# Other places for the tokens' tiles and the weights in the second mixture of experts

## The chip, the cores and the metric

The kernel runs on one core of one Trainium2 chip. What is measured is the device time of one execution, in microseconds (us). The kernel before was run three times; one further execution was profiled, and every row shown here is from that one.

## The reference

Three layers follow one another on 2304 tokens of width 512. The first is attention with a compressive memory, the second a soft mixture of experts, the third a mixture whose gate is balanced by eight rounds of row and column scaling. The change lies in the third, cut here to its core:

```python
P = np.exp(logits - logits.max())        # logits = x @ w_gate, 2304 x 8
for _ in range(8):
    P /= P.sum(1, keepdims=True) + 1e-09
    P /= P.sum(0, keepdims=True) + 1e-09
    P *= N / E
for e in range(8):
    h = np.maximum(x @ w1[e], 0.0)       # 2304x512 @ 512x1024
    out += P[:, e:e + 1] * (h @ w2[e])   # 2304x1024 @ 1024x512
```

## The kernel before

The input `x` of the third layer has rank 32 (it is a mixture of 32 slots), so `layer1` makes the hidden layer of 256 tokens with eight matmuls (L1043, `l<-c4T,a`). Eight experts with nine groups of 256 tokens each are 72 units of work. The first six of expert 0 (`RAW = 6`) go through `plain` (L1327), which multiplies 512 columns at a time, and the other 66 units go through `product`.

In `product` the second matrix product of a unit is done by a Strassen-like scheme: seven products instead of eight, in the order p5, p1, p7, p6, p2, p3, p4. Each takes one token tile (`s1`, `a11`, `s3`, `s2`, `a12`, `s4`, `a22`) and one weight tile (`T1`, `B11`, `T3`, `T2`, `B21`, `B22`, `T4`; the `B` tiles and `T3` lie in the big tiles `BB1` and `BB2`). Each number is split into a high and a low float32r part, names ending in h and l, so a product is 4 steps over the inner dimension times 3 matmuls: high by high (L1360), high by low (L1361), low by high (L1362). That is 84 matmuls of 128x256 for a unit. In each of them the token tile is the stationary operand (loaded by an LDWEIGHTS, which reads 128 columns or 512 bytes of each partition) and the weights are the moving operand (256 columns or 1024 bytes of each partition). The steps of a product lie 512 and 1024 bytes apart, so all 12 matmuls of a product have one and the same distance between their two operands, taken by the remainder by 512.

Places are given out one after another inside a pool: `mA` holds `BB1` and the `T1` and `T2` of even experts, `mB` the token tiles, `mS` small tiles of the gate, `mC` the `T1` and `T2` of odd experts, `BB2` and `T4`, and `mD` the first layer's tiles `a4`. A tile that nobody uses (name "gap") moves all tiles that come after it. The engines' order is written out by hand (`manual_schedule`), and nothing in it depends on places.

Of the kernel before, what the change touches and what calls it, by code (L numbers as in the profile page):

```python
# [8 lines left out]
F32 = mybir.dt.float32  # L9
# [12 lines left out]
def infini_attention_soft_moe_sinkhorn_moe(  # L22
# [22 lines left out]
    P = 128  # L45
# [826 lines left out]
    mA = ctx.enter_context(tc.tile_pool(name="mA", bufs=1, reuse_waits="tile"))  # L872
    mB = ctx.enter_context(tc.tile_pool(name="mB", bufs=1, reuse_waits="tile"))


    mS = ctx.enter_context(tc.tile_pool(name="mS", bufs=1, reuse_waits="tile"))
    mS.tile([P, 24], F32, name="gap")
    mC = ctx.enter_context(tc.tile_pool(name="mC", bufs=1, reuse_waits="tile"))
    mD = ctx.enter_context(tc.tile_pool(name="mD", bufs=1, reuse_waits="tile"))
    ps_l = ctx.enter_context(tc.tile_pool(name="ps_l", bufs=1, space=PSUM, reuse_waits="tile"))  # L880
# [152 lines left out]
    accB = mB.tile([P, NU, DM], F32, name="accB")  # L1033
    accD = mB.tile([P, NU, CW], F32, name="accD")
    units = [(e, u) for e in range(E) for u in range(NU)]
    X, Y, PH, FU = {}, {}, {}, {}

    def layer1(g):
        e, u = units[g]
# [12 lines left out]
    def h_tile(g, nm, z):  # L1052
        if (g, nm, z) not in X:
            tag = ("s3" if nm == "a21" else nm) + z
            X[g, nm, z] = mB.tile([P, KH, P], F32R, tag=tag, name=nm + z)
        return X[g, nm, z]

# [13 lines left out]
    def h_hi(g, nm):  # L1071
        a = nm[0] == "a"
        nc.scalar.activation(  # L1073
            out=h_tile(g, nm, "h"), in_=ph(g, nm) if a else FU[g, nm], func=AF.Relu if a else AF.Copy
        )

    def h_lo(g, nm):
        hi, lo = h_tile(g, nm, "h").bitcast(F32), h_tile(g, nm, "l")
        if nm[0] == "a":
            nc.vector.scalar_tensor_tensor(  # L1080
                out=lo, in0=ph(g, nm), scalar=0.0, in1=hi, op0=ALU.max, op1=ALU.subtract
            )
        else:
            nc.gpsimd.tensor_tensor(out=lo, in0=FU[g, nm], in1=hi, op=ALU.subtract)  # L1084
# [451 lines left out]
```

## Time and profile before

| | |
|---|---|
| median of 3 runs | 1152.31 us (1148.59 to 1152.92) |
| profiled execution, its own time | 1150.51 us |
| its span, first to last instruction | 1148.7 us |
| TensorE (PE) busy | 1096.2 us, 95% of the span |
| VectorE (DVE), ScalarE (ACT), GpSimd (POOL) busy | 853.0, 656.6, 658.7 us |

The profiled execution's own time is 1.8 us above its span and 1.8 us below the median of the three runs. PE's busy time counts matmuls whose ends are modelled and which overlap one another, so how closely they follow each other is read from their starts or their number in a stretch, not from the busy share. The first mixture and the attention end at about 320 us, the six plain units at about 400 us, and the 66 units of seven products fill the rest.

### The profile page before, as it was taken

The page shows a single profiled execution, that of the slowest core. Times are in us where ns is not written, and L with a number is a line of the kernel's source. Part 1 is how long each engine was busy: PE and PEld are TensorE (multiplying, and loading weights), DVE is VectorE, ACT ScalarE, POOL GpSimd, SP SyncE. Part 2 cuts the span into 40 slices and gives each one's busy share as a digit, 9 for nine tenths or more (in the row PEclk, how much of TensorE's full clock was granted, in tenths as well). Part 3 has the DMA queues.
Part 4 walks back from the last instruction along what each step waited for, and adds up shares of the span by engine and source line. Part 5 has one row for each costly group of instructions (what it writes and reads, how often), then busy time and mean ns, then how long its engine had stood idle before and what let it go on. Part 6 is the DMA issues. An engine that isn't in the chain of part 4 may idle for free.

```text
span 1148.7 us, 24354 instructions
## 1 busy us (share of the span) xinstructions
PE 1096.2 (95%) x9247; PEld 992.6 (86%) x9247; DVE 853.0 (74%) x1870; ACT 656.6 (57%) x1423; POOL 658.7 (57%) x602
## 2 busy tenths in 40 slices
PE   5899899988999998999999999999999999999998
PEld 4778777773377888999999999999999999999998
DVE  6888888875146556678778868877887787788776
ACT  6888878751233388556555644655564465556442
POOL 5433323300333287577767857776785877678665
PEclk9999999997999999999999999999999999999999
DMA  6677777238822004001300400120040012000111
GB/s 163 197 205 232 203 224 203 74 123 361 353 74 74 1 2 147 2 2 42 107 2 1 148 2 1 56 93 1 1 148 1 1 68 80 2 1 6 55 53 55
DMA packets 37411, 102.31 MB, mean 89 GB/s; under 512 B 6448, under 2 KB 13232, under 8 KB 33200
## 3 DMA queue, kind: packets, MB, share of 16 engines
q1 hardware_dynamic: 36864, 100.69, 27.1%
q8 instruction: 73, 1.20, 0.4%
q14 instruction: 42, 0.34, 0.1%
q10 hardware_dynamic: 432, 0.09, 0.0%
HBM read 96.04 MB, written 4.72 MB: 88 GB/s over the span
## 4 chain that ended last, share of the span: by engine, by line
PE 71%; DVE 13%; ACT 9%; issue 3%; DMA 2%; POOL 2%; SPq 0%; DVEq 0%; ACTq 0%; POOLq 0%
PE y L1360 15%; PE y L1362 15%; PE y L1361 15%; PE y L1327 5%; PE l L1043 5%; PE po L436 3%; DVE f L1067 2%; PE ph L830 2%; ACT sm L360 2%; PE pt L399 1%; PE pa L999 1%; DVE sm L356 1%; DMA kd<-in_k_dram 1%; DVE a22l L1080 1%; PE pc L1227 1%
## 5 line engine op out<-in xcount | busy, mean ns | idle before, releaser
L1067 DVE SCALAR_TENSOR_TENSOR f<-l,f 128x512 f32<-128x512 f32 x264 | 181.5, 688 | 57.2 <-ACT a11h L1073 50.1
L1084 POOL TENSOR_TENSOR s1l<-f,s1h 128x512 fp32r<-128x512 f32 x66 | 88.5, 1341 | 157.2 <-ACT s1h L1073 153.2
L1376 DVE TENSOR_TENSOR accA<-accA,y 128x512 f32<-128x512 f32 (+1 forms) x129 | 86.7, 672 | 49.2 <-PE y L1362 43.2
L1073 ACT ACTIVATE a12h<-l 128x512 fp32r<-128x512 f32 x72 | 43.2, 600 | 94.0 <-PE y L1362 90.4
L1084 POOL TENSOR_TENSOR s4l<-f,s4h 128x512 fp32r<-128x512 f32 x66 | 85.9, 1302 | 17.4 <-ACT s4h L1073 16.4
L1376 DVE TENSOR_TENSOR accB<-accB,y 128x512 f32<-128x512 f32 x129 | 88.4, 686 | 6.7 <-PE y L1362 1.2
L1084 POOL TENSOR_TENSOR s2l<-f,s2h 128x512 fp32r<-128x512 f32 x66 | 86.1, 1304 | 0.8 <-ACT s2h L1073 0.8
L1043 PE MATMUL l<-c4T,a 128*128 128x256 f32 x576 | 79.0, 280 | 7.5 <-DVE a22l L1080 6.6
L1084 POOL TENSOR_TENSOR s3l<-f,s3h 128x512 fp32r<-128x512 f32 x66 | 85.7, 1299 | 0.3 <-ACT s3h L1073 0.3
L360 ACT ACTIVATE sm<-sm,mn 128x128 f32<-128x128 f32 (+3 forms) x128 | 71.0, 556 | 17.8 <-DVE mn L356 16.3
L1043 PEld LDWEIGHTS l<-c4T,a 128*128 128x128 f32 x576 | 71.6, 188 | 10.4 <-DVE a22l L1080 8.8
L1360 PE MATMUL y<-T2h,s2h 128*128 128x256 f32 x264 | 76.4, 289 | 0.0
L1063 ACT ACTIVATE f<-l 128x512 f32<-128x512 f32 x66 | 39.1, 592 | 65.3 <-PE l L1043 61.9
L969 POOL TENSOR_TENSOR BB1l<-raw,BB1h 128x512 fp32r<-128x512 f32 x32 | 41.1, 1297 | 58.8 <-ACT BB1h L963 55.1
L1361 PE MATMUL y<-BB2l,s4h 128*128 128x256 f32 x264 | 73.8, 279 | 0.3 <-DVE BB2l L969 0.3
L1360 PE MATMUL y<-BB2h,a12h 128*128 128x256 f32 x264 | 73.8, 279 | 0.0
L1362 PE MATMUL y<-BB1h,s3l 128*128 128x256 f32 x264 | 73.3, 278 | 0.1
L1361 PE MATMUL y<-T2l,s2h 128*128 128x256 f32 x264 | 73.4, 278 | 0.0
L1362 PE MATMUL y<-T2h,s2l 128*128 128x256 f32 x264 | 73.3, 278 | 0.0
L1360 PE MATMUL y<-BB2h,s4h 128*128 128x256 f32 x264 | 73.2, 277 | 0.0
L1360 PE MATMUL y<-T4h,a22h 128*128 128x256 f32 x264 | 73.2, 277 | 0.0
L1361 PE MATMUL y<-T4l,a22h 128*128 128x256 f32 x264 | 73.2, 277 | 0.0
(314 smaller groups left out, 4236.1 us busy)
## 6 DMA issues: line engine op xcount, KB each, us to landing
wm<-in_moe_w_dram SPq DMA_DIRECT2D x32, 1024.0 KB, 8.1
raw<-in_moe_w_dram SPq DMA_DIRECT2D x32, 512.0 KB, 4.2
w<-in_moe_w_dram SPq DMA_DIRECT2D x32, 512.0 KB, 4.3
qd<-in_q_dram SPq DMA_DIRECT2D x30, 288.0 KB, 4.2
kd<-in_k_dram SPq DMA_DIRECT2D x30, 288.0 KB, 4.7
qp<-in_q_dram SPq DMA_DIRECT2D x16, 288.0 KB, 3.0
vt<-in_v_dram SPq DMA_DIRECT2D x16, 256.0 KB, 2.7
out_dram<-accB SPq DMA_DIRECT2D x18, 128.0 KB, 1.8
```

Of the source, the lines that this page charges most:

```text
L360: nc.scalar.activation(out=sm[:, 0:n], in_=sm[:, 0:n], func=AF.Exp, scale=-1.0, bias=mnc, accum_out=X.sums[:, i, h : h + 1],)
L969: eng(g).tensor_tensor(out=w_tile(e, nm, "l")[:, h], in0=full(e, nm, i), in1=w_tile(e, nm, "h")[:, h].bitcast(F32), op=ALU.subtract,)
L1043: nc.tensor.matmul(ph[:, f, :], a4s[e][:, P * (KH * j + f) : P * (KH * j + f) + P], c4T[:, UT * u : UT * u + UT], start=True, stop=True,)
L1063: nc.scalar.activation(out=f_tile(g, nm), in_=ph(g, nm), func=AF.Relu)
L1067: nc.vector.scalar_tensor_tensor(out=f_tile(g, nm), in0=ph(g, src), scalar=0.0, in1=b, op0=ALU.max, op1=op)
L1073: nc.scalar.activation(out=h_tile(g, nm, "h"), in_=ph(g, nm) if a else FU[g, nm], func=AF.Relu if a else AF.Copy)
L1084: nc.gpsimd.tensor_tensor(out=lo, in0=FU[g, nm], in1=hi, op=ALU.subtract)
L1327: nc.tensor.matmul(Y[g, i], X[g, f"a{i}{j}", "hhl"[n]][:, f, :], BB[j, "hlh"[n]][:, f].rearrange("p a c -> p (a c)"), start=j == 1 and f = ...
L1360: nc.tensor.matmul(o_, hh[:, f, :], wh[:, f, :], start=f == 0, stop=False)
L1361: nc.tensor.matmul(o_, hh[:, f, :], wl[:, f, :], start=False, stop=False)
L1362: nc.tensor.matmul(o_, hl[:, f, :], wh[:, f, :], start=False, stop=f == KH - 1)
L1376: nc.vector.tensor_tensor(out=acc, in0=acc, in1=y, op=ALU.add)
```

## The change

One unused tile of 96 bytes in `mS` is taken away, and five unused tiles are put between the token tiles: 32 bytes ahead of `s3h`, `a22h`, `s2h` and `s4h`, 128 bytes ahead of `s1h`. Tiles that come later in `mB` move by 32 to 256 bytes, and those of `mS`, `mC` and `mD` by 160.

```diff
-
     mS = ctx.enter_context(tc.tile_pool(name="mS", bufs=1, reuse_waits="tile"))
-    mS.tile([P, 24], F32, name="gap")
...
-    X, Y, PH, FU = {}, {}, {}, {}
+    X, Y, PH, FU, GAPS = {}, {}, {}, {}, {}
...
             tag = ("s3" if nm == "a21" else nm) + z
+
+            n = {"s3h": 32, "a22h": 32, "s1h": 128, "s2h": 32, "s4h": 32}.get(tag, 0)
+            if n and tag not in GAPS:
+                GAPS[tag] = mB.tile([P, n // 4], F32, name=f"gap_{tag}")
             X[g, nm, z] = mB.tile([P, KH, P], F32R, tag=tag, name=nm + z)
```

No engine's row of instructions changes: kinds, order, shapes and semaphore waits are the same, only addresses differ. The addresses give these distances (address of the moving operand less that of the stationary one, remainder by 512 bytes):

| product and operands | before | after |
|---|---|---|
| p5: T1, s1 | 448 | 256 (even experts), 416 (odd) |
| p1: BB1, a11 | 448 | 448 |
| p7: BB1, s3 | 448 | 416 |
| p6: T2, s2 | 448 | 224 (even), 384 (odd) |
| p2: BB2, a12 | 448 | 64 |
| p3: BB2, s4 | 448 | 352 |
| p4: T4, a22 | 448 | 32 |
| first layer: c4T, a4 | 448 | 288 |
| plain units: a11, a21, a12, a22 | 448 | 448, 416, 64, 32 |

In the matmuls that spread the slots (L1025, L1026) the distances were 0, 128, 256 and 384 before and are 96, 224, 352 and 480 after. In the attention nothing moves; there the operands of L354 and L355 stand 0 apart for the first head of a block and 256 for the second, and those of L340 64 or 320.

## Rows read from the trace of the kernel before

**Rows 1.** The page's busy times, granted clock by slice, and chain that ended last.
```profile
PE 1096.2 (95%) x9247; PEld 992.6 (86%) x9247; DVE 853.0 (74%) x1870; ACT 656.6 (57%) x1423; POOL 658.7 (57%) x602
...
PEclk9999999997999999999999999999999999999999
...
PE 71%; DVE 13%; ACT 9%; issue 3%; DMA 2%; POOL 2%; SPq 0%; DVEq 0%; ACTq 0%; POOLq 0%
```

**Rows 2.** Waits of PE from 464 us on: us in total, times, longest.
```profile
PE l L1043 <- DVE a22l L1080: 1.0, 6, 0.2
```

**Rows 3.** Stretches of one expert each, PE alone.
```profile
664.00:764.00 100.00, 99.84 (x888) 1.00 0.14 44
...
1064.00:1149.00 85.00, 81.47 (x692) 0.99 0.15 51
```

**Rows 4.** Two stretches of 40 us, PE alone.
```profile
676.00:716.00 40.00, 40.00 (x355) 1.00 0.01 1
...
1068.00:1108.00 40.00, 40.00 (x342) 1.00 0.16 54
```

**Rows 5.** L1361 in 676:716: duration ns least/median/most.
```profile
L1361 PE MATMUL y<-BB1l,s3h x16: 276/276/276, 677.1 to 709.4; 128*128 128x256 f32 x16
```

**Rows 6.** The same line in 1068:1144.
```profile
L1361 PE MATMUL y<-BB2l,s4h x31: 281/281/281, 1068.0 to 1143.7; 128*128 128x256 f32 x31
```

**Rows 7.** PE's groups of the whole span, shapes apart: busy us, mean ns.
```profile
L1043 PE MATMUL l<-c4T,a 128*128 128x256 f32 x576 | 79.0, 280 | 7.5 <-DVE a22l L1080 6.6 <-DVE a L66 0.9
...
L1360 PE MATMUL y<-T4h,a22h 128*128 128x256 f32 x264 | 73.2, 277 | 0.0
...
L1327 PE MATMUL y<-BB1h,a21l 128*128 128x512 f32 x24 | 9.6, 399 | 0.0
```

**Rows 8.** PE in order of time (start us, us), the first layer after a wait.
```profile
661.47 0.28 PE L1361 MATMUL y<-BB1l,a11h 128*128 128x256 f32 x1
661.58 0.28 PE L1362 MATMUL y<-BB1h,a11l 128*128 128x256 f32 x1
662.02 1.21 PE L1043 MATMUL l<-c4T,a 128*128 128x256 f32 x8 [0.16 <-DVE a22l L1080]
663.07 0.28 PE L1360 MATMUL y<-BB1h,s3h 128*128 128x256 f32 x1
663.18 0.28 PE L1361 MATMUL y<-BB1l,s3h 128*128 128x256 f32 x1
663.30 0.28 PE L1362 MATMUL y<-BB1h,s3l 128*128 128x256 f32 x1
```

**Rows 9.** The same view, the spreading of the slots.
```profile
674.21 0.28 PE L1025 MATMUL p<-ahi,sel 128*128 128x256 f32 x1
674.33 0.28 PE L1026 MATMUL p<-alo,sel 128*128 128x256 f32 x1
674.44 0.28 PE L1025 MATMUL p<-ahi,sel 128*128 128x256 f32 x1
674.56 0.28 PE L1026 MATMUL p<-alo,sel 128*128 128x256 f32 x1
674.67 0.29 PE L1360 MATMUL y<-BB1h,a11h 128*128 128x256 f32 x1
```

**Rows 10.** The same view, scores of one block of the attention.
```profile
70.86 0.35 PE L354 MATMUL ps<-kh,qh 128*128 128x256 f32 x1
71.05 0.28 PE L355 MATMUL ps<-klz,qh 128*128 128x256 f32 x1
71.17 0.28 PE L354 MATMUL ps<-kh,qh 128*128 128x256 f32 x1
71.29 0.28 PE L355 MATMUL ps<-klz,qh 128*128 128x256 f32 x1
```

**Rows 11.** L1360 in 464:1064: duration ns least/median/most.
```profile
L1360 PE MATMUL y<-BB1h,a11h x216: 276/276/286, 474.6 to 1061.4; 128*128 128x256 f32 x108
```

**Rows 12.** PE's groups of the first 250 us: 512 columns in the attention.
```profile
L340 PE MATMUL ps<-klz,qx 128*128 128x512 f32 x32 | 10.0, 394 | 0.0
```

## The prediction

> **What bounds the kernel now.** I read the page first: PE is busy for 95% of the span, and 71% of the chain that ended last is its own work; the granted clock is at the higher of its two levels (2.4 GHz) but for short stretches [rows 1]. The waits of PE come next, since the places of tiles can only matter where PE does not stand still for another reason: from 464 us to the end it waits 1.0 us in all, for VectorE [rows 2]. An expert takes 100.00 us, of which PE is busy for 99.84 [rows 3]. So from there on the time is the number of matmuls by the distance in time from one to the next, and nothing else.
>
> That distance is therefore what the other views were read for. Of two stretches of 40 us, one shows 355 matmuls and the other 342 [rows 4]. A matmul is shown for some 280 ns and overlaps those behind it, so a stretch also counts those that began up to 280 ns ahead of it, about 2.4 of them: 40,000 / 352.6 is 113.4 ns from start to start, and 40,000 / 339.6 is 117.8 ns. Both stretches do the same products with the same distance 448 at the same granted clock. The shown duration follows: 276 ns for all 16 of a group in the first stretch, 281 for all 31 of a group in the second [rows 5, 6], and every other group there reads the same. The shown duration less 163 ns is the step, so rows that give only a mean duration tell which of two levels a group was on. I call 113.4 the low level and 117.8 the high one; they are 4.4 ns apart, or 3.9%.
>
> The reader is to see two things in this. The level is no property of the distance alone, because 448 shows both. And it lasts: the second stretch is 40 us without a change. Which level follows is set where the stream is broken. Before L1043 waits for VectorE the steps are 113 ns; behind the wait the eight matmuls of L1043 take 1.05 us to the next product (the first, after the pause, longer than the others), and the starts of the products go on 0.11 and 0.12 apart, on the high level [rows 8].
>
> **The change, part by part.** No instruction, wait or transfer is added, removed or put elsewhere. The gaps themselves cost nothing: they are addresses that nobody writes. What can change is the step of PE's matmuls, and I cost each group by levels.
>
> 1. The seven products: 66 units by 84 matmuls are 5,544, in 21 groups of 264, one of which is shown [rows 7]. Their mean shown duration is 277 ns in that group and in most others (73.2 us by 264 is 277.3), between one fifth and one quarter of the 5 ns from the low to the high level, so I put 0.23 of them on the high level now. Three of the 21 groups, those of p1, keep distance 448; 18 groups, 4,752 matmuls, get another. No stretch of the trace runs long at another distance with 256 columns, so the price has bounds from both sides. From below: all 4,752 on the low level, 4,752 x 0.23 x 4.4 ns = 4.8 us gained. From above by the levels that last: all on the high level, 4,752 x 0.77 x 4.4 = 16.1 us lost. Still further, there is a third step: the longest of the ordinary matmuls in L1360 shows 286 ns, 123 from start to start [rows 11]. It shows singly, not in stretches; all 4,752 there would lose 4,752 x (122.8 - 114.4) = 40 us.
>
> The nearest rows for other distances are short ones with 256 columns. The spreading of the slots has distances 256, 128, 0 and 384, and its starts are 0.12, 0.11, 0.12 and 0.11 us apart [rows 9]. In the attention the second head of a block (distance 256) takes 0.12 us from L354 to L355, and the first head (distance 0) takes 0.12 from L355 to L354; the 0.19 us of the first L354 is the change of operand kind behind the transposes, not the distance, since L355 at distance 0 does not have it [rows 10]. So of the four kinds of neighbour three lie at the high level or a little above, and one (L1026) nearer the low one. I take three quarters of the moved matmuls on the high level and one quarter on the low one: 4,752 x (0.75 - 0.23) x 4.4 = 10.9 us lost. Against these rows speaks that they are short and stand just behind a break, where 448 too shows the high level; that is why the bound below stays in.
>
> 2. The first layer, 576 matmuls, goes from 448 to 288. Its mean of 280 holds about a dozen long ones behind waits [rows 7]; I put 0.4 of it on the high level now, and three quarters later: 576 x 0.35 x 4.4 = 0.9 us. Ends: 1.0 gained, 1.5 lost.
>
> 3. The plain units: 216 of 288 matmuls with 512 columns move. They show 399 [rows 7], the attention's with 512 columns at distances 64 and 320 show 394 [rows 12]. That is 5 ns at most by 216, 1.1 us gained, and as much lost if it goes the other way; I take nothing.
>
> 4. VectorE, ScalarE and GpSimd read and write the moved tiles. Their durations lie beside PE's work, with at least 20% of each expert idle on the fullest of them by the page's busy shares (VectorE 74% of the span) [rows 1]; a few ns there are hidden. If PE is slower, they have more room, so PE's wait of 1.0 us [rows 2] can only shrink.
>
> The sum is 10.9 + 0.9 = 11.8 us on the profiled execution's 1150.5, which gives 1162.3. The median of the runs shown lies 1.8 us above that execution, so the forecast for the median is 1164.
>
> **A rule of the Trainium skill, weighed.** The Trainium skill's page "SBUF — State Buffer" (Who interferes with whom) gives TensorE two independent read ports for SBUF, one for the moving operand and one for the weight load, and says that PE never waits on anyone. By it no distance could cost anything and the time would stay at 1152. This trace does not bear the second half out fully: the same instructions at the same granted clock show two lasting steps, 113.4 and 117.8 ns [rows 4]; something in reading or loading does cost time, but which operands collide is not shown here, nor that their distance decides.
>
> **The rivals.** *No change.* The level is set by where the stream is broken and by what broke it, and the distance only shifts in time where two reads meet; the stream settles again to the same step. For it: 448 has both levels, and breaks choose between them [rows 8]. Against it: the two levels exist at all, and a product at another distance has to settle anew seven times a unit. The time is 1152, with 3 us either way. The Trainium skill's page "SBUF — State Buffer" leads to the same.
>
> *Faster.* The new distances keep every stretch on the low level, also the last expert, which now lies high to its end [rows 6]. The place is the 66 units, the price 4.8 + 1.0 = 5.8 us, so 1146. It decides if fewer than 0.23 of the moved matmuls are high. Against it: three of four neighbours. No row with 256 columns goes below about 113 ns, so I see no larger gain. [...]
>
> *Much slower.* Some distances put a product on the third step, which is now seen singly [rows 11]. Half of the moved matmuls there and half on the high level: 40 / 2 + 16 / 2 = 28 us, so about 1180; all there 1192. It decides from a third of the moved products on.
>
> **How the numbers follow.** The forecast, between half and all of the moved matmuls on the high level (1158 to 1170), has a chance of 0.50; no change 0.26, faster 0.09, much slower 0.15. About 0.5%, or 5.8 us, is what a measurement of this kernel can tell from no change. Faster by more than that takes nearly the whole of the gain in reach: 0.07. Within it lie the no-change rival, the rest of faster and a small piece of the forecast: 0.31. Slower by more: 0.62. The range for 8 in 10 leaves out most of faster below and the worse half of much slower above: 1148 to 1180.
>
> **What would show it.** If the steps are right, the stretches of one expert grow from 100.0 us to about 101.7 (756 matmuls, 648 of them moved, by 2.3 ns), the last stretch stays nearly as it is, the groups of p1 keep about 277 ns while the moved groups show 279 to 281, and PE still waits for nobody. Groups at 276 throughout with experts of 99 us would show the faster rival; groups at 285 and more the third step. All groups at 277 with both levels in the same places would show that the distance does nothing. The prediction is wrong if a moved group shows a step that no row here has, above 123 or below 113 ns, or if p1 changes as much as the moved groups, since then the neighbours in the stream, not the own distance, set the level.

## The result and the profile after

The changed kernel takes 1166.47 us (median of 4 runs, 1166.0 to 1166.96), the kernel before on the same chip 1151.12; the ratio is 1.0127, with a 95% interval of 1.0102 to 1.0153. The forecast was 1164, in a range of 1148 to 1180, so the way and about the size were right. The profiled execution has a span of 1164.3 us against 1148.7.

The page of the changed kernel, busy time and chain, as in [rows 1]:

```profile
PE 1114.4 (96%) x9247; PEld 1014.6 (87%) x9247; DVE 847.4 (73%) x1870; ACT 656.3 (56%) x1423; POOL 659.0 (57%) x602
...
PEclk9999999997999999999999999999999999999999
...
PE 82%; DVE 8%; ACT 6%; issue 2%; POOL 1%; DMA 1%; SPq 0%; DVEq 0%; ACTq 0%; POOLq 0%
```

The number of instructions and the granted clock are as before; only PE and its weight loads are busy for longer, and PE's share of the last chain rose from 71% to 82%. From 464 us on PE waits for nobody any more (1.0 us before, [rows 2]).

One stretch of 102 us, close to a whole expert, and three of 40 us, PE alone, as in [rows 3, 4]:

```profile
667.00:769.00 102.00, 102.00 (x884) 1.00 0.13 43
...
676.00:716.00 40.00, 40.00 (x342) 1.00 0.01 1
776.00:816.00 40.00, 40.00 (x341) 1.00 0.01 1
1096.00:1136.00 40.00, 40.00 (x342) 1.00 0.16 52
```

The stretch that held 355 matmuls holds 342, and the two others hold 341 and 342: 40,000 / 339.6 is 117.8 ns from start to start, and from the first expert to the last no unit averages less than 117.6. From the start of one expert's first product to the next it is 102.7 us (the starts in the trace, 653.06 to 1063.70 us for four experts), where it was 100.0.

PE's groups of the whole span, busy us and mean ns; each product's high-by-low matmuls (L1363 now, L1361 before), one more row of p1, and the first layer:

```profile
L1041 PE MATMUL l<-c4T,a 128*128 128x256 f32 x576 | 79.6, 280 | 5.5 <-DVE a22l L1082 4.6 <-DVE a L66 0.9
...
L1363 PE MATMUL y<-BB2l,s4h 128*128 128x256 f32 x264 | 74.8, 283 | 0.1
...
L1363 PE MATMUL y<-T1l,s1h 128*128 128x256 f32 x264 | 74.3, 282 | 0.0
...
L1363 PE MATMUL y<-T2l,s2h 128*128 128x256 f32 x264 | 74.1, 281 | 0.0
...
L1363 PE MATMUL y<-BB1l,s3h 128*128 128x256 f32 x264 | 74.0, 280 | 0.0
...
L1363 PE MATMUL y<-BB2l,a12h 128*128 128x256 f32 x264 | 73.7, 279 | 0.0
L1362 PE MATMUL y<-BB1h,a11h 128*128 128x256 f32 x264 | 73.7, 279 | 0.0
L1363 PE MATMUL y<-T4l,a22h 128*128 128x256 f32 x264 | 73.7, 279 | 0.0
...
L1363 PE MATMUL y<-BB1l,a11h 128*128 128x256 f32 x264 | 73.5, 278 | 0.0
```

The groups rose from about 277 [rows 7] to 278 to 283, p1 (`a11`) too, whose distance is unchanged. (The one group that reads more, p6's first matmuls behind the transposes, rose from 289 to 293.) The wait in L1041 fell from 6.6 us in eleven places to 4.6 in five.

How a product's matmuls follow one another shows in order of time. Here is p1 in one unit of an odd expert of the changed kernel (start us, us):

```profile
690.65 0.28 PE L1362 MATMUL y<-BB1h,a11h 128*128 128x256 f32 x1
690.77 0.28 PE L1363 MATMUL y<-BB1l,a11h 128*128 128x256 f32 x1
690.88 0.29 PE L1364 MATMUL y<-BB1h,a11l 128*128 128x256 f32 x1
691.01 0.28 PE L1362 MATMUL y<-BB1h,a11h 128*128 128x256 f32 x1
691.12 0.28 PE L1363 MATMUL y<-BB1l,a11h 128*128 128x256 f32 x1
691.24 0.28 PE L1364 MATMUL y<-BB1h,a11l 128*128 128x256 f32 x1
691.35 0.28 PE L1362 MATMUL y<-BB1h,a11h 128*128 128x256 f32 x1
691.47 0.28 PE L1363 MATMUL y<-BB1l,a11h 128*128 128x256 f32 x1
691.58 0.28 PE L1364 MATMUL y<-BB1h,a11l 128*128 128x256 f32 x1
```

The first five steps are 0.12, 0.11, 0.13, 0.11 and 0.12 (114 to 123 ns in the unrounded starts, 118 on average); from the sixth on they are 113 to 114, the low level, to the last but one. Behind p5 at 416, p1 pays for its neighbour's distance in its first matmuls and then settles. In even experts, where p5 stands at 256, it does not settle:

```profile
598.77 0.28 PE L1362 MATMUL y<-BB1h,a11h 128*128 128x256 f32 x1
598.89 0.28 PE L1363 MATMUL y<-BB1l,a11h 128*128 128x256 f32 x1
599.01 0.28 PE L1364 MATMUL y<-BB1h,a11l 128*128 128x256 f32 x1
...
599.84 0.28 PE L1362 MATMUL y<-BB1h,a11h 128*128 128x256 f32 x1
599.95 0.28 PE L1363 MATMUL y<-BB1l,a11h 128*128 128x256 f32 x1
600.07 0.28 PE L1364 MATMUL y<-BB1h,a11l 128*128 128x256 f32 x1
```

In 27 of the 30 units of even experts p1's steps are 117 to 119 ns up to its last matmul: it lies on the high level of 448 throughout. Its mean is 117.6 in even experts and 115.4 in odd ones (113.6 and 114.5 before). The other products do not reach the low level: p3 (352) repeats 117, 125, 115, 124, 118, 121 to its end, p2 (64) 117 and 118, p4 (32) 118, 120, 113, 116. p7, at 416 in all experts, has two patterns, with a mean of 118.8 in even experts and 117.4 in odd ones.

Below, a product's step is the mean from one start to the next over its matmuls, worked out from the starts in the trace without steps of 140 ns or more (change of operand kind, waits); a quiet unit is one without transposes, spreading or waits in it. Before, the steps of p5, p1, p7, p6, p2, p3 and p4 are 114.4, 114.1, 114.3, 114.9, 114.2, 114.2 and 114.4 (mean 114.37); after, 119.2 in even and 118.9 in odd experts, 116.4, 118.0, 118.0 and 118.8, 117.9, 119.7 and 116.9 (mean 118.06).

### The profile page after: what moved, and what is told of

It reads as the page before. It is cut to its first block, busy times and chain, and to the rows that moved or that the text cites. A ratio compares the mean times of both kernels' runs of the same rounds, so it can differ in the third digit from the quotient of the medians.

```text
span 1164.3 us, 24354 instructions
## 1 busy us (share of the span) xinstructions
PE 1114.4 (96%) x9247; PEld 1014.6 (87%) x9247; DVE 847.4 (73%) x1870; ACT 656.3 (56%) x1423; POOL 659.0 (57%) x602
## 4 chain that ended last, share of the span: by engine, by line
PE 82%; DVE 8%; ACT 6%; issue 2%; POOL 1%; DMA 1%; SPq 0%; DVEq 0%; ACTq 0%; POOLq 0%
PE y L1362 18%; PE y L1364 18%; PE y L1363 18%; PE l L1041 6%; PE y L1329 5%; PE po L436 3%; PE ph L830 2%; ACT sm L360 2%; PE pt L399 2%; PE pa L997 1%; PE pso L848 1%; DVE sm L356 1%; PE pc L1229 1%; PE pma L449 1%; DVE r L463 1%
## 5 line engine op out<-in xcount | busy, mean ns | idle before, releaser
L1041 PE MATMUL l<-c4T,a 128*128 128x256 f32 x576 | 79.6, 280 | 5.5 <-DVE a22l L1082 4.6
L1041 PEld LDWEIGHTS l<-c4T,a 128*128 128x128 f32 x576 | 73.0, 188 | 7.2 <-DVE a22l L1082 5.6
L1363 PE MATMUL y<-BB2l,s4h 128*128 128x256 f32 x264 | 74.8, 283 | 0.1
L1364 PE MATMUL y<-BB2h,s4l 128*128 128x256 f32 x264 | 74.6, 283 | 0.0
L1362 PE MATMUL y<-T1h,s1h 128*128 128x256 f32 x264 | 74.5, 282 | 0.0
L1363 PE MATMUL y<-T1l,s1h 128*128 128x256 f32 x264 | 74.3, 282 | 0.0
L1364 PE MATMUL y<-T1h,s1l 128*128 128x256 f32 x264 | 74.2, 281 | 0.0
```

The lines of the kernel that those rows point to most:

```text
L1041: nc.tensor.matmul(ph[:, f, :], a4s[e][:, P * (KH * j + f) : P * (KH * j + f) + P], c4T[:, UT * u : UT * u + UT], start=True, stop=True,)
L1362: nc.tensor.matmul(o_, hh[:, f, :], wh[:, f, :], start=f == 0, stop=False)
L1363: nc.tensor.matmul(o_, hh[:, f, :], wl[:, f, :], start=False, stop=False)
L1364: nc.tensor.matmul(o_, hl[:, f, :], wh[:, f, :], start=False, stop=f == KH - 1)
```

## The experiments

**One product alone at 352.** Two questions come first: does a product pay for its own distance, or for standing beside products with another?

```diff
-    mS.tile([P, 24], F32, name="gap")
...
+            n = {'s4h': 96}.get(tag, 0)
+            if n and tag not in GAPS:
+                GAPS[tag] = mB.tile([P, n // 4], F32, name=f"gap_{tag}")
...
```

> Only p3's token tile moves, so p3 stands at distance 352 and everything else at 448 as before. Own-distance theory (each product pays for its own distance): p3's 792 matmuls go from about 114.2 ns to about 119.7, the mean that p3 shows at 352 in the changed kernel, 4.4 us; p4 and its followers settle within some four matmuls, about 1 us; about 1156.5 us in all, with the other products at 277 to 278 ns shown. Jump theory (what costs is that neighbouring products differ, whatever the distances): two jumps in every unit throw the whole stream off the low level, all products show 279 to 281, some 10 to 16 us more, 1161 to 1167.

Measured: 1151.41 us, ratio 0.9988 (0.9977 to 0.9999). Both theories gave another time. The groups tell why (p3, p7, p1):

```profile
L1363 PE MATMUL y<-BB2l,s4h 128*128 128x256 f32 x264 | 74.4, 282 | 0.0
L1363 PE MATMUL y<-BB1l,s3h 128*128 128x256 f32 x264 | 73.4, 278 | 0.0
...
L1363 PE MATMUL y<-BB1l,a11h 128*128 128x256 f32 x264 | 72.9, 276 | 0.0
```

p3's step is 119.2, as the own-distance theory has it, 5 ns x 792 = 4 us lost. But the others fell: p1 from 114.1 to 113.5, p7 to 113.6, the first layer from 114.5 to 113.9. The last expert, on 117.8 before, now averages 114.3 in a unit, which is twelve matmuls at 119.7 and the rest at 113.3. So p3 costs its price and breaks the high level in every unit, which gives about as much back.

The edges of p3 also tell which two operands matter. Here are p2's last matmul and p3's first ones, then p3's last and p4's first:

```profile
702.18 0.28 PE L1364 MATMUL y<-BB2h,a12l 128*128 128x256 f32 x1
702.30 0.28 PE L1362 MATMUL y<-BB2h,s4h 128*128 128x256 f32 x1
...
703.62 0.28 PE L1364 MATMUL y<-BB2h,s4l 128*128 128x256 f32 x1
703.73 0.28 PE L1362 MATMUL y<-T4h,a22h 128*128 128x256 f32 x1
703.85 0.28 PE L1363 MATMUL y<-T4l,a22h 128*128 128x256 f32 x1
```

The step from p2's last matmul to p3's first is long (122.8 ns on average over the units), although p2 stands at 448: p3's token tile, which is loaded next, stands at 352 from p2's moving operand. The step from p3's last matmul to p4's first is short (113.9), although p3 stands at 352: p4's token tile stands at 448 from p3's moving operand. So a step goes by the distance from a matmul's moving operand to the stationary operand of the matmul behind it; inside a product that is the product's own distance.

**All products at 352.**

```diff
-    mS.tile([P, 24], F32, name="gap")
...
+            n = {'a11h': 96}.get(tag, 0)
...
```

> All seven products and the plain units at one distance, 352; the first layer stays at 448. Own-distance theory: 5,544 matmuls at about 119.8 ns instead of 114.4, 30 us more, about 1181 us, and every product shows about 282 to 283 ns. Jump theory: no jumps between the products, so they stay at 276 to 278 and the time at 1151 to 1154.

Measured: 1181.44 us, ratio 1.0253 (1.0233 to 1.0273), which is 29 us. The steps of the seven products are 119.6 to 120.0, and no unit from the first to the last averages less than 119.7 or more than 120.3. No jump between products is left, and the price is the full one: the jump theory falls, the own distance is what costs, and 352 has no low level at all.

**All tiles elsewhere, the distances of the products and the first layer kept.** (The products' tiles come to lie 160 bytes on. The first layer's tile comes to lie 2,560 bytes on, which is no move by the remainder by 512; the expectation has 160 for it too.)

```diff
+    mA.tile([P, 40], F32, name="gap")
...
-    mD.tile([P, 16], F32, name="gap")
     a4s = {0: mD.tile([P, FF], F32R, tag="a4", name="a4", bufs=2)}
-    Cw = mD.tile([P, NTT, NS], F32, name="Cw")
```

(`Cw` and a gap of 160 bytes stand ahead of `a4` instead.)

> All distances stay 448, but tokens, weights and the first layer's tiles all move by 160 bytes (by the remainder by 512). Own-distance theory and jump theory: nothing changes, 1151 us with 2 us either way, products at 277. Address theory (the place itself counts, not the distance): products change as in the changed kernel by several ns, 5 us or more.

Measured: 1148.86 us, ratio 0.9975 (0.9958 to 0.9991): not slower, so the place itself is not what the change pays for. It is a little faster: in the profile the products' mean step is 114.06 ns against 114.37, 1.7 us in all, and the quiet units of the last expert average 113.6 instead of 117.8. A second set of runs, below, bears that out.

**A break that should bring the low level.**

```diff
-        for t in range(2 * (u1 - u0)):
+        for t in range(4):
...
-                pc[:, P * t : P * t + P], cs_[e, u0][:, t].rearrange("p a s -> p (a s)"), ident
+                pc[:, P * t : P * t + P], cs_[e, u0][:, t % (2 * (u1 - u0))].rearrange("p a s -> p (a s)"), ident
```

> All places as before; where the scaled mixture weights of an expert's last unit are turned with two transposes, four are issued (the two more write columns that nobody reads). Theory that a break chooses the level: four transposes bring the stream back to the low level in the last expert too, where it is high to the end before, 4.4 ns for some 650 matmuls, 2.9 us less, and up to 1 us less in the six others, against 0.1 us for each pair of transposes added: about 1148 us, and the last expert's products at 276 ns. If the level is set by something else there (the end of the loads for a next expert, the output transfers): the last expert stays at 281 and the time is 0.7 us above before.

Measured: 1158.14 us, ratio 1.0048 (1.0031 to 1.0065), slower where 3 to 4 us less were expected. Stretches of this kernel, in the fourth expert and the last:

```profile
676.00:716.00 40.00, 40.00 (x342) 1.00 0.01 1
...
1096.00:1136.00 40.00, 40.00 (x356) 1.00 0.15 49
```

The last expert went low, as expected (x342 before in 1068:1108, [rows 4]). But the stretch from 676 to 716, low before with 355, went high, and so did about four units in each of five experts. That a break chooses the level is borne out, at the same distance of 448 in all of them; that four transposes choose the low one is not.

**The same in the last expert alone.**

```diff
-        for t in range(2 * (u1 - u0)):
+        for t in range(4 if e == E - 1 else 2 * (u1 - u0)):
```

> As four_transposes, but the two added transposes are issued in the last expert alone; all places and all other breaks are as before. Theory that a break chooses the level and that it then lasts: the six experts ahead read as in the kernel before (most units 113.3 to 115.5 ns), and the last reads 113.3 instead of 117.8 in its last seven units or so, as it did in four_transposes: 7.3 x 84 x 4.4 ns = 2.7 us less, 0.2 us more for the transposes, so a ratio of about 0.998. Rival (the low last expert came from what the earlier experts left behind): the last expert stays at 117.8 and the time is the same or 0.2 us more.

Measured: 1150.86 us, ratio 0.9993 (0.9972 to 1.0014), which does not tell the 2.5 us from nothing. In the profile the last expert is low:

```profile
676.00:716.00 40.00, 40.00 (x355) 1.00 0.01 1
...
1096.00:1136.00 40.00, 40.00 (x355) 1.00 0.15 50
```

But the sixth expert has five units at 117.2 to 117.8 that were low in the profile of before, although up to there the two programs are the same. So which level a break leaves is not fixed by the program alone, and a part of it changes from one execution to the next. With all places as before, that makes two profiles with a low last expert behind four transposes against one with a high last expert behind two.

**One part of the change alone: the 96-byte tile taken away.**

```diff
-    mS.tile([P, 24], F32, name="gap")
```

> One part of the change alone: the 96-byte tile in mS is taken away, no gap is added. p2, p3, p4 stand at 352 in all experts, p5 and p6 at 352 in odd ones, the rest at 448, the first layer at 32. Own-distance theory, from 119.8 ns at 352: odd units 36 x 60 matmuls x 5.4 ns = 11.7 us, even units 30 x 36 x 5.4 = 5.8 us, the first layer 1.4 us, less about 1 us since no high level lasts at 448: 17 to 18 us more, about 1169, and each group at 352 shows 282 to 283 ns. If distances cost what they cost only in company (jumps): a few us, as little as in p3_alone_352.

Measured: 1166.57 us, ratio 1.0112 (1.0078 to 1.0146), 13 us, where 17 to 18 were expected. Four groups, p3 and p4 at 352, p1 and p7 at 448:

```profile
L1360 PE MATMUL y<-BB2l,s4h 128*128 128x256 f32 x264 | 74.6, 283 | 0.1
L1360 PE MATMUL y<-T4l,a22h 128*128 128x256 f32 x264 | 74.5, 282 | 0.0
...
L1360 PE MATMUL y<-BB1l,a11h 128*128 128x256 f32 x264 | 73.2, 277 | 0.0
L1360 PE MATMUL y<-BB1l,s3h 128*128 128x256 f32 x264 | 73.0, 276 | 0.0
```

The products at 352 read 119.0 to 120.0 as expected, and odd experts, with five of them, average 118.2 in a quiet unit against 116.3 in even ones. The mean of all steps is 117.69, so the steps alone make 18 us; part of it comes back in fewer long steps, as in the changed kernel (below): with the first layer, all steps of the profile add up to 15.0 us more than before.

**Distances not seen yet.** Two kernels gave each product another one, for their steps more than for their time. (In the first `Cw` lies in `mS` and the 96-byte gap there is gone; in the second `Pr` lies in `mS` and its gap is 64 bytes.)

```diff
+            n = {'a11h': 128, 's3h': 32, 'a12h': 96, 'a22h': 32, 's1h': 32, 's2h': 32}.get(tag, 0)
...
```

> A look at distances that nothing has shown yet: p1 at 320, p7 at 288, p2 at 192, p4 at 160, p5 at 128, p6 and p3 at 96, the first layer at 448. Own-distance theory: each product has a step of its own between 113.3 and 120 ns that repeats with a short pattern; 448 would be no exception if one of these reads 113.3 too. If every distance but 448 costs something like the seven of the changed kernel (116.9 to 119.7, mean 118.3), the time is about 1151 + 21 = 1172.

```diff
+            n = {'a22h': 32}.get(tag, 0)
...
```

> The same look at 0 (p1, p7, p2) and 480 (p5, p6, p3, p4), the first layer at 448. If nearness to 448 counts, 480 reads low and 0 a little more, and the time is near 1151; if 448 is alone, both read 117 to 120 and the time is about 1170.

Measured: 1166.34 us (ratio 1.0114) and 1172.01 us (1.0163). The steps: 320 117.8, 288 116.9, 192 116.2, 160 117.5, 128 119.2, 96 119.4 and 119.6; 0 119.8 to 119.9, 480 117.8 to 118.6. Nearness to 448 does not count, since 480 reads 118. But a pattern does appear: distances 256 apart read alike, 32 and 288, 64 and 320, 96 and 352, 0 and 256, 128 and 384 (160 and 416 less so: 117.5, and 117.4 to 118.9).

**All products at 192.** If that pattern holds, 192 is the same as 448.

```diff
-    Cw = mD.tile([P, NTT, NS], F32, name="Cw")
+    Cw = mS.tile([P, NTT, NS], F32, name="Cw")
...
+            n = {'a11h': 256}.get(tag, 0)
...
```

> All products and the plain units at 192, the first layer at 448. In the runs so far distances 256 apart read alike (32 and 288 at 116.9, 64 and 320 at 117.8, 96 and 352 at 119.4 to 120, 0 and 256 at 119.3 to 119.9). Theory that the remainder by 256 counts: 192 is the same as 448, the products have the two lasting levels 113.3 and 117.8, and the time is 1151, within 4 us for which stretch gets which level. Theory that the remainder by 512 counts, as the change and the forecast have it: 192 keeps its 116.2 of the mixed run in which it stood between other distances, 10 us more, about 1161.

Measured: 1154.21 us, ratio 1.0003 (0.9989 to 1.0018), no change. Both lasting levels are there, the first of these stretches high, the other two low:

```profile
676.00:716.00 40.00, 40.00 (x342) 1.00 0.00 1
...
796.00:816.00 20.00, 20.00 (x179) 1.00 0.00 1
1096.00:1136.00 40.00, 40.00 (x356) 1.00 0.16 53
```

The 116.2 that 192 showed in company was a mean that hid the same two levels: in that kernel, the first of the two above, p2 lies at about 117.8 in 28 of the 66 units, at 114.2 in 24 (113.3 without its last step) and between them in 14. For the good distance the remainder by 256 counts, not by 512.

**The first layer alone at 288, and p3 alone at 288.** One more part of the change, and the cheaper distance for p3.

```diff
-    mD.tile([P, 16], F32, name="gap")
+    mD.tile([P, 56], F32, name="gap")
```

> One part of the change alone: the first layer's tile goes to 288, all products stay at 448. Own-distance theory with levels that a break chooses: its eight matmuls in each unit cost 2.3 to 3.4 ns each, 1.3 to 1.8 us, and the first four or so of p7 behind it settle, 1.2 us; but the first layer now breaks every unit, so no high level lasts beyond a unit, which gives back up to 5.7 us of what the high stretches cost: 1148 to 1151. If a jump leads to the high level: up to 1165.

```diff
-    mS.tile([P, 24], F32, name="gap")
+    mS.tile([P, 48], F32, name="gap")
...
-    Cw = mD.tile([P, NTT, NS], F32, name="Cw")
+    Cw = mS.tile([P, NTT, NS], F32, name="Cw")
...
+            n = {'s4h': 160}.get(tag, 0)
...
```

> As p3_alone_352 but p3 at 288, whose own step is 116.9 instead of 119.7. Own-distance theory: 792 x 2.8 ns = 2.2 us less than p3_alone_352, about 1149.5, with all units near 114.0 and no lasting high level. If the step at 288 is no property of the distance: the same 1151.4 as p3_alone_352.

Measured: 1149.79 us, ratio 0.9962 (0.9950 to 0.9975), and 1150.31, ratio 0.9962 (0.9949 to 0.9976), with 1154.8 for the kernel before on that chip. p3 and p1 of the second kernel:

```profile
L1364 PE MATMUL y<-BB2l,s4h 128*128 128x256 f32 x264 | 74.5, 282 | 0.3 <-DVE BB2l L969 0.3
...
L1364 PE MATMUL y<-BB1l,a11h 128*128 128x256 f32 x264 | 72.9, 276 | 0.0
```

(The mean of 282 for p3 holds some long steps; its step without them is 116.4.) In both kernels one piece of work at another distance breaks the stream once in every unit, the rest stays low (113.4 or 113.8 in a quiet unit, the last expert included), and the mean step is 113.84 and 114.19 against 114.37 before. The first layer's own step is 116.3, near the 116.8 of the changed kernel. The profiles show only a part of the gain: the steps of the products and the first layer add up to 1.3 and 1.5 us less than in the profile of before, while the ratios stand for 4.4 us. The kernel before was not profiled again on that chip, so where the rest comes from stays open.

**The moved tiles again.**

> all_moved_160 once more beside the others, with more rounds: its mean step over the products was 114.06 ns against 114.37 before, 1.7 us, and it ended 2.6 us earlier in the trace. If that is a property of the program (which break leaves which level), the ratio is again 0.997 to 0.998 and the units repeat; if it is the luck of one execution, the ratio is 1.000.

Measured: 1149.92 us, ratio 0.9965 (0.9948 to 0.9982); mean step 113.96, and most units repeat those of the first profile to 0.1 ns. All products stand at 448 here, but p1's moving operand stands 96, not 448, from the first layer's tile, which is loaded behind it, and the first layer's moving operand 288 from the token tile of p7. These two steps of a unit take 123.4 and 117.6 ns, as at the edges of p3. So a break in every unit would explain the gain as in the two kernels above; that was not tried by itself. These three kernels beat the kernel before by about 0.35%, and by their ratios to it the changed one by about 1.6%.

## Why the prediction came out right, step by step

- **What bounds the kernel.** Right: the time followed PE's stream alone. All steps of the products and the first layer, long ones included, add up to 717.0 us before and 733.0 after; these 16.0 us are the span's 15.6.
- **Term 1, the seven products, 10.9 us.** Mis-sized. Their steps rose by 3.69 ns on average (118.06 less 114.37), 20 us over some 5,470, not by 2.3 ns in 4,752. Two things were missing. The moved products have no mix of two levels, as the forecast put it (three quarters high, one quarter low); each distance has short patterns of its own, with means from 116.9 to 119.7. And p1, which was to keep 277 ns, went from 114.1 to 116.4, 1.8 us. Of these, 1.4 us come from even experts, where p1 stays on its high level behind p5, and 0.4 from odd ones, where it settles within some five steps. The text ahead named that as a sign that the neighbours set the level; the runs show that both count, the own distance for which steps a product can have and the neighbour for how it begins and, at 448, on which level it goes on. The neighbours that the share of three quarters was read from point the right way, but the four matmuls of [rows 9] stand at 0, 384, 384 and 256, so 128 is not among them.
- **What came back.** 4.8 us in the products, which no term had: their long steps, of 140 ns and more, fell from 79 (24.8 us) to 57 (17.4). The largest part are the steps just ahead of the first layer, with its waits for VectorE: 9.7 us in eleven before, 6.0 in five now, as PE comes later. The forecast said that this wait can only shrink, but from 464 us on, where it was 1.0 us; the larger waits stand ahead of that. So the forecast of 11.8 us stood near the 15.4 (the medians; 15.6 in the profiled spans) partly because two omissions had opposite signs.
- **Term 2, the first layer, 0.9 us.** Its ordinary steps rose from 114.5 to 116.8, 1.3 us; with fewer long ones 0.6 is left. So this term came out near for the same two opposite reasons.
- **Term 3, the plain units, nothing.** Right: 62.3 us of ordinary steps before, 62.1 after; at 512 columns the means lie between 230.9 and 233.8 ns.
- **Signs named ahead.** An expert was to take 101.7 us (the prediction's 648 matmuls by 2.3 ns make 101.5) and takes 102.7; the last was to stay as it is and does (342 matmuls in 40 us before and after); the moved groups were to show 279 to 281 and show 279 to 283; no group came to the third step, though single steps of 125 ns repeat in p3.
- **The rivals.** No change is refuted by the steps at 352: with nothing else changed, they cost 29 us of 1152. By the Trainium skill's page "SBUF — State Buffer" (Who interferes with whom), with two independent read ports for PE's moving operand and its weight load, no distance should cost anything; the runs disagree for these matmuls, and the measurement decides. Faster could not come from the seven new distances, since none of them showed the low level. Much slower would take all products at 352 or 0: 1181 is the measured end, not 1192.
- **Levels and breaks.** Right that 448 has two lasting levels and that a break chooses; the last expert was low in both profiles in which only a break was changed. Which break leads to which level stays open, and some of it differs between executions. How much of the spread of the times this makes is not shown: four runs of before spread over 4.3 us and four of the changed kernel over 1.0, but four with all products at 352, which have one level, over 4.0.

Why a distance has the pattern that it has, and why one remainder has two levels, no run here shows. That the stationary operand of the next matmul is the one that matters is read from the edges of p3 and of the first layer; no run was made for it.

## What to carry to other kernels

Where PE never waits, read its starts one by one: a mean of 277 ns hid two lasting levels 3.9% apart, and the placing of operands was worth up to 2.5%. Keep all neighbours in a stream of 128x256 float32r matmuls at one good distance, and look what happens behind each break; a small piece of work at another distance can even pay (0.4% here), and in the profiles the high level then does not last. A uniform kernel for one distance told more than a mixture, in which a mean such as 116.2 for 192 can once more hide two levels.

## What the runs showed of the hardware that was not expected

Steps of float32r matmuls of 128x256, weights loaded for each, at the granted clock of 1.00 (distance: moving less stationary operand; ns):

| distance | step | distance + 256 | step |
|---|---|---|---|
| 0 | 119.8 to 119.9 | 256 | 119.2 |
| 32 | 116.5 to 116.9 | 288 | 116.3 to 116.9 |
| 64 | 117.9 | 320 | 117.8 |
| 96 | 119.4 to 119.6 | 352 | 119.0 to 120.0 |
| 128 | 119.2 | 384 | 118.8 |
| 160 | 117.5 | 416 | 117.4, or 118.8 to 118.9 |
| 192 | 113.3 or 117.8, lasting | 448 | 113.3 or 117.8, lasting |
| 224 | 118.0 | 480 | 117.8 to 118.6 |

Only the 192 row has a low level, and only in it two levels were seen to last for tens of us; 416 too showed two patterns. Except for 192, 352 and 448 these are steps in company of other distances, so a part of each is settling. At 512 columns the distance hardly shows: about 233 ns at 448 and at 352 over the plain units. And the distance that counts is that from a matmul's moving operand to the stationary operand of the next matmul: with 448 on both sides, a single step at 96 between them took 123.4 ns and one at 288 took 117.6.
